# w_in's columns dealt to partitions in runs of four, w_out in two transfers of 8 KB runs, alpha loaded in place

## The chip, the cores and the metric

The kernel runs on one core of one Trainium2 chip. The metric is the device time of one execution in microseconds; the given figure is the median of three runs. A profiled execution of the same kernel gives the trace that is read below.

## The reference

A sparse attention (a window of 32 to each side, and 8 global tokens that see all and are seen by all) is followed by a feed-forward layer with the snake activation. B is 8, there are 8 heads of 64, 576 tokens in each batch element, d_model is 512 and d_ff is 2048.

```python
scores = scale * (q @ k.T)                  # scale = 1 / sqrt(64)
mask = (abs(pos[:, None] - pos[None, :]) <= 32) | is_global[:, None] | is_global[None, :]
attn = softmax(where(mask, scores, -1e9))
x = (attn @ v).transpose(0, 2, 1, 3).reshape(4608, 512)
h = x @ w_in                                # 512 x 2048
g = h + sin(alpha * h) ** 2 / (alpha + 1e-9)
out = g @ w_out                             # 2048 x 512, float32 out
```

All inputs are float32, the indices int64. The kernel computes in bf16 with float32 accumulation.

## The kernel before

The eight batch elements go through three steps each: `attention(b)`, `gemm1(b)` (x times w_in, then the activation) and `gemm2(b)` (the result times w_out, then the store). The order of the instructions on each engine is the order of the program text: nothing is rescheduled. gemm2's matmuls are a generator, and `fill(n)` takes n of them into the stream of PE between the matmuls of the next element's attention and gemm1.

The hidden dimension d_ff is cut into 16 groups of 128, `nt`. In gemm1 a group takes 8 matmuls: 4 chunks `c` of d_model by two halves of the tokens, each with its own weight load of w_in (L992), 288 columns wide (320 for the last element). ACT then computes the sine with `alphaT[:, nt]` as its scale (L1022), ACT or DVE squares it, and DVE adds it to h into `H2` (L1030). gemm2 loads 128 tokens of `H2` as weights and streams 512 columns of `w_out[:, nt]` (L1049).

The weights come in through POOL's queue, which converts float32 to bf16 on the way: `load_w_in` in four quarters of 512 columns (L411; two at the start, two in the first attention step), and `load_w_out` in four transfers of four groups each (L417), issued in gemm1 of element 0 at group 11. Behind `load_w_out` on POOL stand the cast of the global V rows (L696), the copies of the global keys and queries of element 1 into `KX` and `QX` (L372, L377), and the loads of V (L394). A DMA waits until the one eight places ahead of it on its queue has landed.

The hidden unit that group `nt` holds at partition p is `nt * 128 + p`: w_in's columns of a group lie side by side, w_out's rows of a group are 128 rows in order, 2 KB apart in DRAM. `alpha` is loaded by SP as 16 rows of 128 (`arow`, L483), turned by PE (L680) and copied to `alphaT` by ACT (L684). SP's queue goes on with reading the eight indices into registers, gathering the global rows of k (L489), loading the global V rows of element 0 (L403), gathering q, and turning k and q of element 1 (L340). The DVE makes `recipT` from `alphaT` (L1119).

Near the end the kernel judges whether the fast path's limits held: ACT squares w_in (L890), DVE adds the squares into `W2`, PE sums `W2` over its partitions with 16 matmuls of one column (L897, the column norms). At the end the verdict is read into registers by all engines, POOL stores the global rows with an indirect DMA (L1083), 54 matmuls into banks that nothing reads follow on PE (L1199), and each engine jumps over a general path (L1206) that this input does not take.

Of the kernel before, what the change touches and what calls it, by code (L numbers as in the profile page):

```python
# [11 lines left out]
AF = mybir.ActivationFunctionType  # L12
DT = mybir.dt
# [3 lines left out]
P = 128  # L17
# [3 lines left out]
WCOL = 120  # L21
# [5 lines left out]
QROW = QLEN + 2 * PAD  # L27
CUT = 3 * SEG
PLACES = [(w, t, y) for w in (1, 0) for t in range(2) for y in range(2)]
LIM_SUM = float(2.0**50)  # L30
LIM_REC = float(2.0**40)
TINY = float(2.0**-60)
LIM_ARG2 = 9.3


def general_path(tc, q, k, v, global_idx, out, w_in, w_out, alphaT, recipT):


    nc = tc.nc
    B, H, S, D = q.shape  # L40
    NKT = S // KW
    NT = alphaT.shape[1]
    CT = w_in.shape[1]
    DM = w_out.shape[2]
    HALF = S // 2
    WIN = 32
# [7 lines left out]
    with ExitStack() as gx:  # L54
# [4 lines left out]
        idf = one.tile([P, P], DT.float32, name="g_idf")  # L59
# [5 lines left out]
            out=g64[:],  # L65
            in_=bass.AP(tensor=global_idx.tensor, offset=global_idx.offset, ap=[[0, P], [1, NG]]),
# [13 lines left out]
        for j in range(NG):  # L80
            for at, acc in ((pos, colg), (row, rowg)):
                nc.vector.scalar_tensor_tensor(
                    out=acc[:], in0=at[:], scalar=gf[:, j : j + 1], in1=acc[:],
# [5 lines left out]
        for i in range(NKT):  # L89
            for sgn in (1, -1):  # L90
                nc.gpsimd.affine_select(
                    out=MQ[:, i, :], in_=MQ[:, i, :], compare_op=ALU.is_ge, fill=0.0,
# [3 lines left out]
                out=MQ[:, i, :], in0=MQ[:, i, :], scalar1=rowg[0:KW, i : i + 1], scalar2=None,  # L96
# [4 lines left out]
            out=NEG[:], in0=MQ[:], scalar1=1.0, scalar2=1.0e9, op0=ALU.subtract, op1=ALU.mult  # L101
# [5 lines left out]
        with tc.For_i(0, B, 1) as b:  # L107
            for hp in range(H // 2):
                nat = []
                for src, name in ((q, "g_Qn"), (k, "g_Kn"), (v, "g_Vn")):  # L110
                    t = wk.tile([KW, NKT, 2, D], DT.float32, name=name)
                    for h in range(2):
                        nc.sync.dma_start(
                            out=t[:, :, h, :],
                            in_=src[bass.ds(b, 1), 2 * hp + h].rearrange("o (j p) d -> p (o j) d", p=KW),
# [6 lines left out]
                for src, name in ((Qn, "g_qT"), (Kn, "g_kT")):  # L122
                    pt = ps.tile([P, 2, 512], DT.float32, name="g_pt")
                    for i in range(NKT):
                        nc.tensor.transpose(
                            out=pt[:, i // 3, (i % 3) * KW : (i % 3 + 1) * KW],
                            in_=src[:, i, :, :], identity=idf[0:KW, 0:KW],
                        )
                    t = wk.tile([P, S], DT.float32, name=name)
# [6 lines left out]
                for h in range(2):  # L136
                    lo = h * D
                    for i in range(NKT):
                        sp = ps.tile([KW, 2, 512], DT.float32, name="g_sp")
                        for e in range(2):  # L140
                            nc.tensor.matmul(
                                out=sp[:, e, 0:HALF],
# [52 lines left out]
            for nt in range(NT):  # L195
                hg = ps.tile([P, 2, 512], DT.float32, name="g_pt")
                for c in range(CT):
                    for e in range(2):
                        nc.tensor.matmul(
                            out=hg[:, e, 0:HALF], lhsT=w_in[:, c, nt * P : (nt + 1) * P],  # L200
                            rhs=xT[:, c, e * HALF : (e + 1) * HALF],
                            start=(c == 0), stop=(c == CT - 1),
                        )
                y = wk.tile([P, 2, HALF], DT.float32, name="g_y")
                n = wk.tile([P, 2, HALF], DT.float32, name="g_n")
                nc.vector.tensor_scalar(
                    out=y[:], in0=hg[:, :, 0:HALF], scalar1=alphaT[:, nt : nt + 1], scalar2=None,
                    op0=ALU.mult,
                )
                nc.vector.tensor_scalar(  # L210
                    out=n[:], in0=y[:], scalar1=1.0 / TWO_PI, scalar2=None, op0=ALU.mult
                )
                for m in (MAGIC, -MAGIC):
                    nc.vector.tensor_scalar(out=n[:], in0=n[:], scalar1=m, scalar2=None, op0=ALU.add)
                for part in (hi, mid, low):
                    nc.vector.scalar_tensor_tensor(
                        out=y[:], in0=n[:], scalar=-part, in1=y[:], op0=ALU.mult, op1=ALU.add
                    )
                edge = float(np.nextafter(np.float32(np.pi), np.float32(0)))
                nc.vector.tensor_scalar(  # L220
                    out=y[:], in0=y[:], scalar1=edge, scalar2=-edge, op0=ALU.min, op1=ALU.max
                )
                nc.scalar.activation(out=y[:], in_=y[:], func=AF.Sin)
                nc.vector.tensor_tensor(out=y[:], in0=y[:], in1=y[:], op=ALU.mult)
                nc.vector.scalar_tensor_tensor(
                    out=HB[:, nt, :].rearrange("p (e c) -> p e c", e=2),
                    in0=y[:], scalar=recipT[:, nt : nt + 1], in1=hg[:, :, 0:HALF],
                    op0=ALU.mult, op1=ALU.add,
                )
# [18 lines left out]
def kernel(  # L248
# [23 lines left out]
    assert global_idx.shape[0] == NG and NT12 == 12  # L272

    const = ctx.enter_context(tc.tile_pool(name="const", bufs=1))
    w_in = const.tile([P, CT, DFF], DT.bfloat16, name="w_in")
    w_out = const.tile([P, NT, DM], DT.bfloat16, name="w_out")
    alphaT = const.tile([P, NT], DT.float32, name="alphaT")
    recipT = const.tile([P, NT], DT.float32, name="recipT")
# [128 lines left out]

    def load_w_in(gs):
        for g in gs:
            cols = slice(g * DFF // 4, (g + 1) * DFF // 4)  # L410
            nc.gpsimd.dma_start(  # L411
                out=w_in[:, :, cols], in_=moe_w_in[:, cols].rearrange("(c p) n -> p c n", p=P)
            )

    def load_w_out():
        for g in range(4):
            nc.gpsimd.dma_start(  # L417
                out=w_out[:, 4 * g : 4 * g + 4, :],
                in_=moe_w_out[4 * g * P : (4 * g + 4) * P, :].rearrange("(t p) n -> p t n", p=P),
            )  # L420


# [49 lines left out]
        out=g64[:],  # L472
        in_=bass.AP(tensor=global_idx.tensor, offset=global_idx.offset, ap=[[1, NG], [0, B], [1, 1]]),
    )
    arow = setup.tile([NT, P], DT.float32, name="arow")
    nc.sync.dma_start(out=girow[:], in_=global_idx[None, :])
    for t in (0, D):
        nc.sync.dma_start(out=gp64[t + KT : t + KT + NG], in_=global_idx[:, None])
# [1 line left out]
            out=gidx8[t + KT : t + KT + NG],  # L480
            in_=bass.AP(tensor=global_idx.tensor, offset=global_idx.offset, ap=[[0, NG], [1, NG]]),
        )
    nc.sync.dma_start(out=arow[:], in_=moe_alpha.rearrange("(t p) -> t p", p=P))  # L483
    gi32 = girow[:].bitcast(DT.int32)
    greg = [nc.sync.value_load(gi32[0:1, 2 * j : 2 * j + 1], min_val=0, max_val=S - 1) for j in range(NG)]

# [188 lines left out]
    for w, name in ((1, "k"), (0, "q")):  # L675
# [1 line left out]
        nc.tensor.transpose(  # L677
            out=pg[w][:], in_=g0[name][:], identity=identb[0 : NG * B, 0 : NG * B]
        )
    nc.tensor.transpose(out=both[:, 0:NT], in_=arow[:], identity=idf[0:NT, 0:NT])  # L680
    for t in range(2):
        place_global_keys(t, act)
        place_global_queries(t, act)
    act(out=alphaT[:], in_=both[:, 0:NT])  # L684
    turn_part(0, 1, views([z[:] for z in zo]))
    turn_part(1, 1, views([zn[:, n, :] for n in range(2)]))
    def second_half():
# [199 lines left out]
    def square_w(c):  # L887

        t = KX[0][:].rearrange("p h i c -> p (h i c)")[:, (c - 1) * DFF : c * DFF] if c else W2[:]
        nc.scalar.activation(out=t, in_=w_in[:, c, :], func=AF.Square)  # L890
        if c:
            nc.vector.tensor_tensor(out=W2[:], in0=W2[:], in1=t, op=ALU.add)

    def column_norms(pw):

        for nt in range(NT):
            nc.tensor.matmul(  # L897
                out=pw[:, nt : nt + 1], lhsT=W2[:, nt * P : (nt + 1) * P], rhs=ones[:, 0:1],
                start=True, stop=True, skip_group_check=True,
            )  # L900
        c2 = normp.tile([P, NT], DT.float32, name="c2")
        nc.vector.tensor_tensor(out=c2[:], in0=alphaT[:], in1=alphaT[:], op=ALU.mult)
        nc.vector.tensor_tensor(out=c2[:], in0=pw[:, 0:NT], in1=c2[:], op=ALU.mult)
        nc.vector.tensor_reduce(out=limit[:], in_=c2[:], axis=AX.X, op=ALU.max)
        nc.vector.tensor_scalar(
            out=limit[:], in0=limit[:], scalar1=1e-30, scalar2=1.0 / LIM_ARG2, op0=ALU.max, op1=ALU.mult
        )
        nc.vector.reciprocal(out=limit[:], in_=limit[:])
# [60 lines left out]
    def gemm1(b):  # L969
# [11 lines left out]
        def chunks(nt, cs):  # L981
            if nt not in hs:
                if order[nt] == "o":
                    hs[nt] = [(slice(e, e + 1), zo[e][:, None, :]) for e in range(2)]
                else:
                    h = {"n": zn, "d": zd}.get(order[nt]) or hr.tile([P, 2, 512], DT.float32, name="zr")
                    hs[nt] = [(slice(0, 2), h[:])]
            h = [ap[:, i] for es, ap in hs[nt] for i in range(es.stop - es.start)]
            for c in cs:
                for e in range(2):  # L990
                    lhsT = w_in[:, c, nt * P : (nt + 1) * P]
                    nc.tensor.matmul(  # L992
                        out=h[e][:, 0:W], lhsT=lhsT, rhs=xT[:, c, e, 0:W],
                        start=(c == 0), stop=(c == CT - 1), skip_group_check=True,
                    )
# [195 lines left out]
    verdicts = judge(zn[:, 0, :])  # L1191
    next(verdicts)
    sure = gemm2_globals(verdicts)
    tiles = [(r, c) for r in (0, D) for c in (0, D)]
    for kinds, n in ((tiles, 6), (tiles[0:2], 6), (tiles[0::3], 6), ([None], 6)):
        for i in range(n):
            for at in kinds:
                rows, cols = (slice(0, P), slice(0, P)) if at is None else [slice(x, x + D) for x in at]
                nc.tensor.matmul(  # L1199
                    out=(zn if len(kinds) == 2 else zd)[cols, (rows.start or 0) // D, 0:WCOL],  # L1200
                    lhsT=VX[0][rows, 0, i, cols], rhs=H2[rows, i, 0:WCOL],
                    start=True, stop=True, skip_group_check=True,
                )
    mctx.close()

    with tc.If(sure < P, preferred_fallthrough_block=False):  # L1206
# [31 lines left out]
```

## Time and profile before

| | |
|---|---|
| median of 3 runs | 366.73 us (366.41 to 366.94) |
| the profiled execution's own time | 366.15 us |
| its span, first to last instruction | 364.4 us |
| mean granted clock of TensorE | 0.993 |
| PE / ACT / DVE / POOL busy | 338.4 / 293.5 / 283.3 / 139.2 us |
| weight loads of w_in (L992) | 1024, 98 ns each |
| w_in, w_out: transfers | 4 and 4, 512 KB each as written |

In the profile, PE is the matmuls and PEld the weight loads, which overlap the matmuls; the ends of matmuls are modelled, so the distance between starts says more than a single duration. A name such as `zo<-w_out,H` says what is written and what is read. "idle before" is the time in which the engine stood still ahead of an instruction, with what ended it; "issue" means that nothing in the profile explains it. The lines with `SPq` or `POOLq` are instructions of a queue. A line's number is that of the kernel before.

### The profile page before, as it was taken

What the parts mean: (1) busy time and instruction counts of PE and PEld (TensorE: products, weight loads), DVE (VectorE), ACT (ScalarE), POOL (GpSimd) and SP (SyncE); (2) the same over time, 40 slices, a digit from 0 to 9 for tenths busy, and PEclk for the clock granted to TensorE, in tenths of its full rate; (3) what the DMA queues carried; (4) which work ended last, traced back from release to release, by engine and by line L of the source; (5) the groups of instructions that cost most, each with busy time, mean ns of one, the idle gap of its engine ahead of it and who ended that gap; (6) DMA issues with size and microseconds to landing.
All of it is one profiled execution on the core that took longest, in us unless ns stands there. A gap on an engine that the chain in (4) does not pass through costs nothing. (4 is left out here: it accounts for less than half of the span.)

```text
span 364.4 us, 8575 instructions
## 1 busy us (share of the span) xinstructions
PE 338.4 (93%) x3110; PEld 230.8 (63%) x3110; DVE 283.3 (78%) x623; ACT 293.5 (81%) x566; POOL 139.2 (38%) x246
## 2 busy tenths in 40 slices
PE   2579978999999999999999999999999999999994
PEld 1467656766567666776666766766676766655453
DVE  6776998588988877888888887888788866798661
ACT  7689997886978788887888897979888888878711
POOL 7992686669874702661066304730000000000001
PEclk9999998999999999999999999999999999999999
DMA  7997999999999783989199904647120011000321
GB/s 118 120 171 162 181 146 189 156 168 198 146 237 202 73 123 81 172 89 161 31 158 120 149 29 50 68 50 148 43 59 29 2 31 60 29 3 0 105 70 53
DMA packets 103580, 38.07 MB, mean 104 GB/s; under 512 B 94139, under 2 KB 98251, under 8 KB 103083
## 3 DMA queue, kind: packets, MB, share of 16 engines
q0 software_dynamic: 56640, 18.56, 44.6%
q1 hardware_dynamic: 46890, 18.89, 25.5%
q8 instruction: 26, 0.43, 0.5%
q14 instruction: 24, 0.19, 0.2%
HBM read 37.15 MB, written 17.83 MB: 151 GB/s over the span
## 5 line engine op out<-in xcount | busy, mean ns | idle before, releaser
L1049 PE MATMUL zo<-w_out,H 128*128 128x512 bf16 x576 | 153.7, 379 | 0.0
L992 PEld LDWEIGHTS <-w_in 128*128 128x128 bf16 x1024 | 98.6, 98 | 45.6 <-issue 9.1
L394 POOL DMA_DIRECT2D VX<-in_v_dram x128 | 83.3, 659 | 89.8 <-PE zd L784 62.9
L1049 PEld LDWEIGHTS <-H 128*128 128x128 bf16 x576 | 52.3, 97 | 37.2
L750 ACT ACTIVATE E<-ring 128x480 bf16<-128x480 f32 x96 | 54.2, 567 | 22.6 <-PE ring L742 22.2
L753 DVE TENSOR_TENSOR E<-E,MASK 128x480 bf16<-128x480 bf16 x96 | 36.0, 405 | 16.9 <-ACT E L750 15.5
L1083 POOL DMA_INDIRECT out_dram<-osb,ghalf x1 | 1.1, 1067 | 119.6 <-POOLq L1206 119.6
L1030 DVE SCALAR_TENSOR_TENSOR H<-s,recipT,zn 128x576 bf16<-128x576 bf16 x47 | 38.2, 814 | 10.3 <-ACT s L1026 6.5
L1026 ACT ACTIVATE s<-sb 128x576 bf16<-128x576 bf16 (+1 forms) x62 | 42.7, 689 | 2.0
L742 PE MATMUL ring<-QX,KX 128*128 128x120 bf16 x384 | 38.0, 225 | 6.5 <-ACT E L750 3.0
L742 PEld LDWEIGHTS <-KX 128*128 128x128 bf16 x384 | 29.0, 102 | 22.0 <-issue 8.8
L1022 ACT ACTIVATE sb<-zn,alphaT 128x576 bf16<-128x576 f32 (+1 forms) x47 | 34.7, 739 | 9.8 <-PE zn L992 9.7
L1030 DVE SCALAR_TENSOR_TENSOR H<-s,recipT,zd 128x576 bf16<-128x576 bf16 x39 | 31.7, 814 | 6.5 <-ACT s L1026 4.7
L1030 DVE SCALAR_TENSOR_TENSOR H<-s,recipT,zr 128x576 bf16<-128x576 bf16 x39 | 31.7, 813 | 4.5 <-ACT s L1026 2.4
L1022 ACT ACTIVATE sb<-zd,alphaT 128x576 bf16<-128x576 f32 (+1 forms) x39 | 28.9, 740 | 7.1 <-PE zd L992 5.8
L1028 DVE TENSOR_TENSOR s<-sb 128x576 bf16<-128x576 bf16 (+1 forms) x66 | 30.7, 465 | 4.1 <-ACT sb L1022 3.6
L1022 ACT ACTIVATE sb<-zr,alphaT 128x576 bf16<-128x576 f32 (+1 forms) x39 | 28.9, 740 | 5.6 <-PE zr L992 5.4
L784 PEld LDWEIGHTS <-VX 128*128 128x128 bf16 x448 | 26.6, 100 | 9.4 <-issue 3.5
L1055 ACT COPY osb<-zo 128x512 f32<-128x512 f32 x36 | 20.8, 577 | 11.3 <-PE zo L1049 10.0
L992 PE MATMUL zn<-xlast,w_in 128*128 128x288 bf16 (+1 forms) x192 | 28.8, 289 | 0.3
L992 PE MATMUL zn<-xT,w_in 128*128 128x288 bf16 x184 | 26.9, 286 | 2.3 <-DVE H L1030 0.9
L784 PE MATMUL zn<-E,VX 128*128 128x120 bf16 (+2 forms) x336 | 26.9, 211 | 1.0 <-DVE xlast L816 0.9
(163 smaller groups left out, 492.6 us busy)
## 6 DMA issues: line engine op xcount, KB each, us to landing
VX<-in_v_dram POOLq DMA_DIRECT2D x128, 36.0 KB, 5.4
kd<-in_k_dram POOLq DMA_DIRECT2D x7, 576.0 KB, 7.1
qd<-in_q_dram POOLq DMA_DIRECT2D x7, 576.0 KB, 10.1
w_in<-in_moe_w_in_dram POOLq DMA_DIRECT2D x4, 512.0 KB, 6.0
w_out<-in_moe_w_out_dram POOLq DMA_DIRECT2D x4, 512.0 KB, 7.8
out_dram<-osb SPq DMA_DIRECT2D x8, 256.0 KB
out_dram<-osb SPq DMA_DIRECT2D x8, 224.0 KB
out_dram<-osb SPq DMA_DIRECT2D x8, 192.0 KB
```

The lines of the kernel that those rows point to most:

```text
L394: nc.gpsimd.dma_start(out=VX[b % 2][r : r + 24, hp, :, t * D : t * D + D], in_=v[b, 2 * hp + t].rearrange("(i a y) d -> y a i d", a=24, y= ...
L742: nc.tensor.matmul(out=ps[:, e * WCOL : (e + 1) * WCOL], lhsT=kx[:, hp, i, :], rhs=qx[:, hp, :, s0 : s0 + 60], start=True, stop=True, skip ...
L750: nc.scalar.activation(out=Eg, in_=ps[:, 0 : 4 * WCOL], func=AF.Exp, scale=scale, accum_out=EA[:, n : n + 1])
L753: nc.vector.tensor_tensor(out=Eg, in0=Eg, in1=MASK[:, 4 * g : 4 * g + 4, :].rearrange("p i c -> p (i c)"), op=ALU.mult,)
L784: nc.tensor.matmul(out=out_t[:, half, :, a - half * CUT : z - half * CUT], lhsT=OB[:] if key else VXb[:, hp, i, :], rhs=E[:, i, :, a - s0 ...
L992: nc.tensor.matmul(out=h[e][:, 0:W], lhsT=lhsT, rhs=xT[:, c, e, 0:W], start=(c == 0), stop=(c == CT - 1), skip_group_check=True,)
L1022: nc.scalar.activation(out=sb[:, es, 0:W], in_=h[:, :, 0:W], func=AF.Sin, scale=alphaT[:, nt : nt + 1])
L1026: nc.scalar.activation(out=s2[:, :, 0:W], in_=sb[:, :, 0:W], func=AF.Square)
L1028: nc.vector.tensor_tensor(out=s2[:, :, 0:W], in0=sb[:, :, 0:W], in1=sb[:, :, 0:W], op=ALU.mult)
L1030: nc.vector.scalar_tensor_tensor(out=H2[:, nt, r0 : r0 + S].rearrange("p (e c) -> p e c", e=2)[:, es], in0=s2[:, es, 0:HALF], scalar=recip ...
L1049: nc.tensor.matmul(out=ops[:], lhsT=H2[:, nt, blk * P : (blk + 1) * P], rhs=w_out[:, nt, :], start=(nt == 0), stop=(nt == NT - 1),)
L1055: nc.scalar.copy(out=osb[:], in_=ops[:])
```

## The change

There are four edits.

- Partition p of group `nt` now holds the hidden unit `512 * (nt // 4) + 4 * p + nt % 4`. A weight load of w_in takes every fourth column of a quarter (`columns(nt)`), and the tile of w_in is laid out quarter by quarter, `[P, 4, CT, 512]`, each quarter's load writing one block. The square of w_in, the column norms and the general path follow the new layout.
- `load_w_out` takes two transfers in place of four. A partition's four rows of a quarter lie side by side in DRAM, so a run is 8 KB as read and 4 KB as written.
- `alpha` is loaded straight into `alphaT`, in runs of four values; the tile `arow`, its transposition on PE and the copy on ACT go.
- The 54 matmuls ahead of the end of the program are left out.

```diff
+RUN = 4
+def columns(nt):
+    return slice(nt % RUN, nt % RUN + RUN * 127 + 1, RUN)
...
-    w_in = const.tile([P, CT, DFF], DT.bfloat16, name="w_in")
+    w_in = const.tile([P, NT // RUN, CT, RUN * P], DT.bfloat16, name="w_in")
...
     def load_w_in(gs):
         for g in gs:
-            cols = slice(g * DFF // 4, (g + 1) * DFF // 4)
             nc.gpsimd.dma_start(
-                out=w_in[:, :, cols], in_=moe_w_in[:, cols].rearrange("(c p) n -> p c n", p=P)
+                out=w_in[:, g],
+                in_=moe_w_in[:, g * RUN * P : (g + 1) * RUN * P].rearrange("(c p) n -> p c n", p=P),
             )
     def load_w_out():
-        for g in range(4):
+        for half in range(2):
+            rows = slice(half * DFF // 2, (half + 1) * DFF // 2)
             nc.gpsimd.dma_start(
-                out=w_out[:, 4 * g : 4 * g + 4, :],
-                in_=moe_w_out[4 * g * P : (4 * g + 4) * P, :].rearrange("(t p) n -> p t n", p=P),
+                out=w_out[:, half * NT // 2 : (half + 1) * NT // 2, :].rearrange("p (g t) n -> p g (t n)", t=RUN),
+                in_=moe_w_out[rows].rearrange("(g p t) n -> p g (t n)", p=P, t=RUN),
             )
...
-    arow = setup.tile([NT, P], DT.float32, name="arow")
...
-    nc.sync.dma_start(out=arow[:], in_=moe_alpha.rearrange("(t p) -> t p", p=P))
+    nc.sync.dma_start(
+        out=alphaT[:].rearrange("p (g t) -> p g t", t=RUN),
+        in_=moe_alpha.rearrange("(g p t) -> p g t", p=P, t=RUN),
+    )
...
-    nc.tensor.transpose(out=both[:, 0:NT], in_=arow[:], identity=idf[0:NT, 0:NT])
...
-    act(out=alphaT[:], in_=both[:, 0:NT])
...
     def square_w(c):
-        nc.scalar.activation(out=t, in_=w_in[:, c, :], func=AF.Square)
+        nc.scalar.activation(out=t.rearrange("p (g n) -> p g n", n=RUN * P), in_=w_in[:, :, c, :], func=AF.Square)
...
-                out=pw[:, nt : nt + 1], lhsT=W2[:, nt * P : (nt + 1) * P], rhs=ones[:, 0:1],
+                out=pw[:, nt : nt + 1], lhsT=W2[:, nt // RUN * RUN * P :][:, columns(nt)], rhs=ones[:, 0:1],
...
     def gemm1(b):
-                    lhsT = w_in[:, c, nt * P : (nt + 1) * P]
+                    lhsT = w_in[:, nt // RUN, c, columns(nt)]
...
     sure = gemm2_globals(verdicts)
-    tiles = [(r, c) for r in (0, D) for c in (0, D)]
-    for kinds, n in ((tiles, 6), (tiles[0:2], 6), (tiles[0::3], 6), ([None], 6)):
-        for i in range(n):
-            for at in kinds:
-                rows, cols = (slice(0, P), slice(0, P)) if at is None else [slice(x, x + D) for x in at]
-                nc.tensor.matmul(
-                    out=(zn if len(kinds) == 2 else zd)[cols, (rows.start or 0) // D, 0:WCOL],
-                    lhsT=VX[0][rows, 0, i, cols], rhs=H2[rows, i, 0:WCOL],
-                    start=True, stop=True, skip_group_check=True,
-                )
     mctx.close()
```

More of the change, by code (lines that the diff above doesn't have):

```diff
@@ L42, in general_path @@
     NT = alphaT.shape[1]
-    CT = w_in.shape[1]
+    CT = w_in.shape[2]
     DM = w_out.shape[2]
@@ L199, in general_path @@
                         nc.tensor.matmul(
-                            out=hg[:, e, 0:HALF], lhsT=w_in[:, c, nt * P : (nt + 1) * P],
+                            out=hg[:, e, 0:HALF], lhsT=w_in[:, nt // RUN, c, columns(nt)],
                             rhs=xT[:, c, e * HALF : (e + 1) * HALF],
```

## The prediction

> **What bounds the kernel now.** I read the page first, then the busy times by stretch, then the groups of instructions by form, and then the timeline around each place that the change touches.
>
> ```profile
> span 364.4 us, 8575 instructions
> ...
> PE 338.4 (93%) x3110; PEld 230.8 (63%) x3110; DVE 283.3 (78%) x623; ACT 293.5 (81%) x566; POOL 139.2 (38%) x246
> ...
> q1 hardware_dynamic: 46890, 18.89, 25.5%
> ...
> L992 PEld LDWEIGHTS <-w_in 128*128 128x128 bf16 x1024 | 98.6, 98 | 45.6 <-issue 9.1
> ```
> ```profile
> 52.50:60.50 8.00, 5.75 (x61) 4.44 (x62) 7.56 (x21) 6.35 (x15) 6.30 (x12) 0.79 1.33 197
> 60.50:333.00 272.50, 269.79 (x2443) 183.19 (x2440) 219.37 (x446) 229.43 (x447) 92.52 (x169) 1.00 0.67 98
> ```
>
> The columns of the second fence are the stretch, its length, the busy time of PE, PEld, DVE, ACT and POOL, the granted clock, the share of the DMA engines and GB/s. From 60.5 to 333 us PE is busy for 269.8 of 272.5 us at full clock: there the matmul stream is the bound, and only what lengthens PE's stream, or makes it wait, moves the end. Ahead of 60.5 us it is the chain of loads, ACT and DVE. So each part is priced by one question: does it touch PE's stream, or the chain of the first 60 us, or the tail?
>
> **The change part by part.** *Weight loads with a step.* 1024 weight loads of w_in now take columns that lie 4 elements (8 bytes) apart. A weight load lies beside the matmul ahead of it, so its room is the distance between two matmuls.
>
> ```profile
> L992 PE MATMUL zr<-xT,w_in 128*128 128x288 bf16 x152 | 22.4, 286 | 0.0
> ...
> L704 PEld LDWEIGHTS zo<-idf,H 64*128 64x128 f32 x8 | 0.6, 138 | 0.2 <-issue 0.2
> ...
> L897 PE MATMUL zn<-ones,W 128*128 128x1 bf16 x16 | 0.5, 163 | 0.0
> ```
> ```profile
> 45.72 0.57 PEld L704 LDWEIGHTS zo<-idf,H 64*128 64x128 f32 x8 [0.24 <-issue]
> ...
> 287.44 1.14 PE L992 MATMUL zn<-xT,w_in 128*128 128x288 bf16 x8
> ...
> 347.05 0.54 PE L897 MATMUL zn<-ones,W 128*128 128x1 bf16 x16
> ```
> ```profile
>   issue: 9.1, 31
> ...
>   DVE HG L1036: 3.4, 10
> ```
>
> Eight matmuls of 288 columns take 1.14 us, the last one 0.286: they start (1.14 - 0.286) / 7 = 122 ns apart. That is a load's room. What a load occupies when nothing hides it shows in the column norms, whose matmuls have one column: (0.54 - 0.163) / 15 = 25 ns apart, load included. No row has a load with a step. The slowest load here is the f32 one of L704: (0.57 - 0.138) / 7 = 62 ns apart. So the ends are 25 and 62 ns; both are far below 122, and inside gemm1 the cost is 0 either way. It shows in two places only. The 16 loads of the column norms have no cover and stand in PE's stream ahead of the last of gemm2: 0 to 16 x (62 - 25) ns = 0.6 us. And where PE begins again after a wait, the first load's length may be seen: the third fence counts 31 such waits on "issue" and 10 on HG for the loads of w_in, at 0 to 138 - 98 = 40 ns each, so 0 to 1.6 us. I take 0 for both: the stepped load has the type, the rows and the column count of the 25 ns load, and only the step is new.
>
> [...] No row here shows a step.
>
> *alpha in place.* SP now issues 512 runs of 16 bytes in place of 16 runs of 512; one PE transpose and one small ACT copy go.
>
> ```profile
> 3.46 0.32 SPq L483 DMA_DIRECT2D arow<-in_moe_alpha_dram  x1
> ...
> 16.02 0.17 DVE L1119 TENSOR_SCALAR recipT<-alphaT 128x16 f32<-128x16 f32 x1
> ...
> 16.14 0.96 PE L742 MATMUL ring<-QX,KX 128*128 128x120 bf16 x8 [1.45 <-DVE QX L612]
> ...
> 21.84 8.06 SPq L489 DMA_DIRECT2D H<-in_q_dram  x8
> ...
> 32.26 2.16 SPq L340 DMA_TRANSPOSE kt<-kd  x1
> ...
> 42.68 1.15 PE L992 MATMUL zn<-xT,w_in 128*128 128x288 bf16 x8 [0.79 <-DMA w_in<-in_moe_w_in_dram]
> ...
> 43.87 0.74 ACT L1022 ACTIVATE sb<-zn,alphaT 128x576 bf16<-128x576 f32 x1
> ```
> ```profile
> SPq L340 <- DMA kd<-in_k_dram: 3.3, 1, 3.3
> ```
>
> The removed copy saves nothing: the first scores at 16.14 waited for DVE's QX. The new wait is DVE's L1119, first needed at 16.02, over 12 us after the issue; behind it on DVE are the first masks. What is queued behind alpha on SP: eight register loads, three gathers, the loads of the global V rows and the transposes of k and q. SP is done with the gathers at 21.84 + 8.06 = 29.90 and issues the transpose at 32.26 after a wait, so it has 2.36 us to spare. The issue's price: in the low case by the transposes. Of q1's 46890 packets some 12300 are counted in the code for outputs, gathers and global rows, the other 34600 belong to 14 transposes, 2470 each in 2.16 us, so 512 runs add 0.45 us. In the high case by the gathers, 64 runs in 8.06 / 8 = 1.0 us: 8 us. I take the low one, as 128 partitions spread like the transposes' rows, and it is under the 2.36. The packets themselves: q1's mean is 0.255 x 364.4 x 16 / 46890 = 32 ns, so 512 take 512 x 32 / 16 = 1.0 us of all engines, while k, q and V stream in. A delay there passes by way of kd, the transposes and the third load of w_in to the PE wait at 42.68, and ACT's sine at 43.87 follows it at once. Between 0 and 1.0 us; I take 0.2, as most of it falls before V's loads fill the queue.
>
> *w_out in two transfers.* POOL issues two transfers of 256 runs in place of four of 512.
>
> ```profile
> 46.85 3.08 POOL L417 DMA_DIRECT2D w_out<-in_moe_w_out_dram x4 [0.23 <-DMA VX<-in_v_dram]
> ...
> 49.65 0.42 DVE L708 CAST kTg<-zo 128x256 bf16<-128x256 f32 x1
> ...
> 50.48 3.13 POOL L372 COPY KX<-kTg 64x96 bf16<-64x96 bf16 x8
> ...
> 53.84 1.28 ACT L726 ACT_TABLE_LOAD   x1
> ...
> 54.42 0.37 PE L742 MATMUL ring<-QX,KX 128*128 128x120 bf16 x4 [1.96 <-POOL QX L377]
> ...
> 55.14 0.57 ACT L750 ACTIVATE E<-ring 128x480 bf16<-128x480 f32 x1
> ...
> 60.56 0.59 PE L1049 MATMUL zo<-w_out,H 128*128 128x512 bf16 x2
> ...
> 61.20 0.64 POOL L394 DMA_DIRECT2D VX<-in_v_dram  x1 [2.22 <-DMA w_out<-in_moe_w_out_dram]
> ```
>
> POOL saves about 3.08 / 2 = 1.5 us. Behind it stand the copies of the global keys and queries, for which PE waits 1.96 us at 54.42: it looks like a gain of 1.5. But the copies need kTg, which DVE writes until 49.65 + 0.42 = 50.07, so they start at most 50.48 - 50.07 = 0.4 us earlier. And what is late next is ACT: its first exp starts at 55.14, right when the table load ends (53.84 + 1.28 = 55.12), though its scores were done by 54.42 + 0.37 = 54.79. So the path gains 0; bounds -0.4 and 0. The weights are first used at 60.56, and the last of four transfers had landed by 61.20, so the first of two halves is there with room: 0. w_in's loads keep their runs; the squares on ACT keep their sizes: 0.
>
> *The tail.* 54 matmuls that nothing reads go from PE's end.
>
> ```profile
> 356.43 0.35 SPq L1062 DMA_DIRECT2D out_dram<-osb  x1
> ```
> ```profile
> 358.96 0.49 PE L1199 MATMUL zd<-H,VX 128*128 128x120 bf16 x6
> 359.60 1.07 POOL L1083 DMA_INDIRECT out_dram<-osb,ghalf  x1 [119.64 <-POOLq L1206]
> ```
> ```profile
> L1206 PEldq COMPARE_BRANCH  x1: 3297/3297/3297, 359.6 to 359.6; - x1
> ```
> ```profile
> q14 instruction: 3, 0.02, 6.6%
> q0 software_dynamic: 2, 0.00, 1.3%
> ```
> ```profile
> DMA to landing us min/median/max: 3.2/3.2/3.2
> ```
>
> What ends last is POOL's store of the global rows, 359.60 + 3.2 = 362.8, and then the closing semaphores. POOL's queue waits for the earlier stores, the last of which SP issues at 356.43, not for these matmuls: removing them moves the store by 0. But PE's jump over the other path (3.3 us from 359.6, while its code is fetched) starts when they end at 359.45, and would start over a microsecond earlier. The fourth fence is the DMA traffic from 361.8 to 363 us: the store's last two packets run beside three packets of instructions. With PE's fetch out of the way the landing can be 0 to 362.8 - 361.8 = 1.0 us earlier. I take -0.4, near the middle.
>
> **Sum** against the profiled execution, 366.15 us (span 364.4 and 1.75 around it): 0 + 0.2 + 0 - 0.4 = -0.2, so 365.95. The median of the runs is 366.73; with the same difference 366.5. Less than 0.2% (0.73 us) is about what a measurement of this kernel can tell from no change.
>
> **The rivals.** *A: the step takes the fast load away (slower).* Place: the column norms and PE's restarts in gemm1. Price: 0.6 + 1.6 = 2.2 us on top of -0.2, up to 368.7. It decides once a stepped load occupies clearly more than 25 ns. For: f32 loads show 62 against 25 ns. Against: same type and column count. *B: the stepped load is longer than its room.* Beyond 122 ns each further ns costs 1024 ns; at 140 ns it is 18 us, 385. Against: no load here occupies even 63 ns. *C: alpha holds SP.* Beyond 2.36 us of issue everything to the third load of w_in slides; the high case, 8 - 0.3 - 2.4, gives +5.3, 371.8. *D: faster.* The second fence shows a mean clock of 0.79 from 52.5 to 60.5 us, after PE's wait at 54.42. If POOL's 0.4 us keep PE awake, up to 8 x (1 - 0.79) = 1.7 us of slow clock go; with the landing's full 1.0 us the time is near 365. *E: the halves don't land sooner and nothing else moves:* that is the forecast within its bounds.
>
> **How the numbers follow.** Forecast (with E) 0.48, its own range 365.8 to 367.3; A 0.24; B 0.07; C 0.06; D 0.15. A, B and C are slower: 0.37. D and the forecast's lower edge are faster: 0.15 + 0.04 = 0.19. Same: 0.44. The range goes from D's 365.0 to A's 368.8 and leaves out B, most of C and D's far side.
>
> **What would show it.** Right: loads of w_in start 122 ns apart as before and PE is busy as before from 60 to 333 us; the norms' 16 matmuls in 0.54 us; w_out's two issues near 1.5 us in total, and ACT's first exp of the second batch still right behind its table load; PE's jump near 358.5; the last landing 0 to 1 us sooner after the store. Wrong: matmuls of gemm1 further apart than 122 ns (B), the norms longer by 0.6 us (A), the transpose issued after 32.7 (C), a full clock in the stretch from 52 to 60 us (D).

## The result and the profile after

The changed kernel takes 370.88 us (median of 4 runs, 369.97 to 371.24) against 366.57 us for the kernel before (median of 4, 365.97 to 366.94): a ratio of 1.0115, 95% interval 1.0092 to 1.0139. It is 4.3 us slower, outside the predicted range. The profiled execution took 371.24 us, of which 369.5 is the span.

The page of the kernel after, and three groups of instructions of the kinds that the prediction priced (busy us, mean ns of one, idle time before them):

```profile
span 369.5 us, 8461 instructions
...
PE 338.5 (92%) x3055; PEld 245.7 (67%) x3055; DVE 284.1 (77%) x623; ACT 293.2 (79%) x565; POOL 137.7 (37%) x244
...
PEclk9999995899999999999999999999999999999998
...
L999 PEld LDWEIGHTS <-w_in 128*128 128x128 bf16 x1024 | 114.8, 114 | 32.1 <-issue 7.5
...
L424 POOL DMA_DIRECT2D w_out<-in_moe_w_out_dram x2 | 1.4, 718 | 0.1
...
L904 PE MATMUL zn<-ones,W 128*128 128x1 bf16 x16 | 0.7, 171 | 0.0
```

PE is busy for as long as before (338.5 and 338.4 us), although the 54 matmuls at the end, 1.54 us of it before, are left out. So the other matmuls took some 1.7 us longer, and the rest of the 5.1 us more of span is waiting. Placing the same instruction in both traces tells where: the first scores start 0.25 us later than before, the first products of element 1 (`zn<-E,VX`) 2.6 us, the first gemm2 matmul 3.8 us, the last one 4.7 us. Most of it arises between 54 and 65 us. The timeline of the kernel after shows the chain there, with the wait ahead of an instruction in brackets:

```profile
47.19 1.43 POOL L424 DMA_DIRECT2D w_out<-in_moe_w_out_dram  x2
...
54.32 0.37 PE L749 MATMUL ring<-QX,KX 128*128 128x120 bf16 x4 [1.64 <-POOL QX L383]
...
60.92 0.53 PE L791 MATMUL zn<-E,VX 128*128 128x88 bf16 x4 [2.30 <-DMA VX<-VGb]
...
63.06 0.57 ACT L757 ACTIVATE E<-ring 128x480 bf16<-128x480 f32 x1 [4.17 <-PE ring L749]
...
64.39 1.06 PE L1056 MATMUL zo<-w_out,H 128*128 128x512 bf16 x2
```

Before, the same products started without a wait:

```profile
58.28 0.58 PE L784 MATMUL zn<-E,VX 128*128 128x88 bf16 x4
```

`VX<-VGb` is SP's load of the global V rows of element 1, many packets of 128 bytes on queue q1, while w_out comes in on POOL's queue q0. The DMA view from 55 to 58 us, inside w_out's transfer, gives each queue's packets, MB and share of the 16 engines' time; first the kernel before, then the kernel after:

```profile
q0 software_dynamic: 596, 0.59, 117.9%
q1 hardware_dynamic: 284, 0.03, 15.0%
```
```profile
q0 software_dynamic: 151, 0.61, 103.9%
q1 hardware_dynamic: 74, 0.01, 4.0%
```

w_out moves the same bytes (0.59 and 0.61 MB), but in packets of 4096 bytes written in place of 1024. By its record one of them takes 1.039 x 48 / 151 = 0.33 us, before 1.179 x 48 / 596 = 0.095 us (48 is 3 us of 16 engines; the shares add up to more than 100%, so records overlap and these times are a little too long). The small packets fell by the same factor, 284 to 74: in both kernels there are two of w_out's packets to one of theirs, whatever the size.

The trace of the kernel after suggests why it is two. The landing of each small load has 8 reports, that of each w_out transfer 16, read here as one from each engine. In the window 70 of the 71 starts of packets of 128 bytes are followed within 10 ns by the start of one of w_out's, and 80 of w_out's follow none. That reads as one to one on half of the engines, with w_out alone on the others; the engines themselves are inferred, as the trace at hand doesn't name a packet's engine.

That is the theory for the experiments, called W: the two queues take turns on an engine by packet, so four times longer packets on one queue leave the other a quarter of its rate. It is the author's reading of the 284 and 74 small packets; no row shows a turn by itself.

The second thing that the windows show is the clock (the column after POOL). The first row is the kernel before, the other two are the kernel after:

```profile
60.50:67.00 6.50, 5.57 (x65) 3.63 (x62) 3.88 (x11) 5.42 (x17) 5.09 (x9) 1.00 1.52 187
```
```profile
60.50:67.00 6.50, 6.08 (x49) 4.49 (x50) 2.45 (x8) 3.28 (x9) 4.29 (x7) 0.51 1.40 182
...
56.61:66.85 10.24, 7.94 (x58) 5.33 (x56) 6.07 (x19) 5.28 (x17) 6.39 (x11) 0.50 1.36 184
```

From 56.61 to 66.85 us PE ran at half clock, 10.24 us in a row; before, half clock lasted 3.41 us (55.67 to 59.08). In this trace the wait and the slow clock lie together, and the experiments have to part them.

### The profile page after: what moved, and what is told of

It reads as the page before. It is cut to its first block, busy times and chain, and to the rows that moved or that the text cites. A ratio compares the mean times of both kernels' runs of the same rounds, so it can differ in the third digit from the quotient of the medians.

```text
span 369.5 us, 8461 instructions
## 1 busy us (share of the span) xinstructions
PE 338.5 (92%) x3055; PEld 245.7 (67%) x3055; DVE 284.1 (77%) x623; ACT 293.2 (79%) x565; POOL 137.7 (37%) x244
## 3 DMA queue, kind: packets, MB, share of 16 engines
q1 hardware_dynamic: 47386, 18.89, 25.4%
## 5 line engine op out<-in xcount | busy, mean ns | idle before, releaser
L999 PEld LDWEIGHTS <-w_in 128*128 128x128 bf16 x1024 | 114.8, 114 | 32.1 <-issue 7.5
```

The costliest lines, as they stand in the source:

```text
L999: nc.tensor.matmul(out=h[e][:, 0:W], lhsT=lhsT, rhs=xT[:, c, e, 0:W], start=(c == 0), stop=(c == CT - 1), skip_group_check=True,)
```

## Experiments

The rivals to W: S, the stepped weight loads; A, alpha's small pieces; the clock by itself; the tail. Each kernel is compared with the kernel before on the same chip, so ratios count and not single times.

**w_out's transfers alone.**

```diff
 (the kernel before)
-        for g in range(4):      # 2 KB runs, four transfers
+        for half in range(2):   # 8 KB runs, two transfers, as in the change
...
```

> The kernel before with one part of the change, load_w_out in two transfers of 8 KB runs; w_in's columns stay as before, so the rows of w_out that meet an element of zn are not its own, and only the time is read. Theory W (w_out's packets of 4096 B and the small packets of SP's loads of the global values take turns on each DMA engine, so that the small ones fall from 284 to 74 between 55 and 58 us, and PE waits for them): the whole loss is here, 370.0 to 371.0 us against 366.6, some 75 small packets in 55 to 58, and PE waits of 2 to 3 us for VX<-VGb ahead of zn<-E,VX near 58 to 61. Rival S (the stepped weight loads of gemm1 and the norms cost it): 366.3 to 366.9 here. Rival A (alpha's load in 2048 pieces holds SP or the DMA engines): the same, 366.3 to 366.9.

Ratio 1.0131 (1.0107 to 1.0154), 371.22 against 366.35 us: the whole loss, a little more than expected, without any other part of the change. The DMA view from 55 to 58 us and the timeline:

```profile
q0 software_dynamic: 168, 0.62, 104.4%
q1 hardware_dynamic: 75, 0.01, 3.9%
```
```profile
61.45 0.53 PE L786 MATMUL zn<-E,VX 128*128 128x88 bf16 x4 [3.05 <-DMA VX<-in_v_dram]
```

75 small packets, as expected. PE waits 3.05 us at the same place. The releaser is named as V's own load here and `VX<-VGb` in the kernel after; both write `VX`, and the name is only what ended last by the profile. What speaks for VGb is the time of its packets: the first 192 of them (heads 0 and 1) have started by 60.73 us here and by 60.03 in the kernel after, 0.7 and 0.9 us ahead of the products; before it was 57.08 us. SP's own queue is closer still: its tenth load waits for the second, that of head 1, to land (the last report is 0.02 us ahead of the tenth's issue, in the kernel before and in the kernel after). It is issued at 61.33 us here and at 60.80 in the kernel after, and the products start 0.12 us later both times (before: 57.67, and the products 0.61 us later). The pieces of V that land here at the same time belong to head pairs 2 and 3 (`load_v(1, (2, 3))`), which these products don't read.

**The steps alone.**

```diff
 (the kernel before)
-                    lhsT = w_in[:, c, nt * P : (nt + 1) * P]
+                    lhsT = w_in[:, nt // RUN, c, columns(nt)]
...
```

> The kernel before with w_in held quarter by quarter and its columns taken in steps of four, in gemm1 and in the norms; w_out, alpha and the last matmuls stay as before, so the elements of zn don't meet their own rows of w_out or their own alpha, and only the time is read. Theory W: 366.5 to 367.0 against 366.6: gemm1's matmuls still start 122 ns apart though the loads take 114 ns instead of 98, and only the norms' 16 matmuls grow by some 8 ns each. Rival S: 369.5 to 371, the whole loss.

Ratio 1.0028 (1.0003 to 1.0052): 0.1 to 1.9 us. Its profiled span is 364.6 us against 364.4, at the low end of this (it was the fastest of the twelve executions), and the last gemm2 matmul starts 0.3 us later than before. The steps cost little, by these numbers not nothing; they aren't the loss.

**Everything of the change, but w_out in four transfers again, with packets as small as before.**

```diff
 (the kernel after)
-        for half in range(2):
+        for t in range(RUN):
...
-                out=w_out[:, half * NT // 2 : (half + 1) * NT // 2, :].rearrange("p (g t) n -> p g (t n)", t=RUN),
-                in_=moe_w_out[rows].rearrange("(g p t) n -> p g (t n)", p=P, t=RUN),
+                out=w_out[:].rearrange("p (g t) n -> p t g n", t=RUN)[:, t],
+                in_=moe_w_out.rearrange("(g p t) n -> t p g n", p=P, t=RUN)[t],
```

> The kernel after with w_out in four transfers of 2 KB runs, one for each step of four rows, everything else as after. Theory W: the packets are again 1024 B written, the small ones come back to 250 to 290 in 55 to 58 us, PE's wait for VX<-VGb goes, and the time is 366.5 to 367.3, where up to 0.7 us may be left if a gemm2 matmul now waits for the fourth transfer. Rivals S and A: 370.5 to 371.2, as after.

Ratio 0.9993 (0.9975 to 1.0012): the loss is gone, with the steps, alpha and the shorter tail still in. The DMA view from 55 to 58 us, and the products, which start without a wait:

```profile
q0 software_dynamic: 601, 0.60, 118.8%
q1 hardware_dynamic: 283, 0.03, 14.9%
```
```profile
57.38 0.36 PE L788 MATMUL zn<-E,VX 128*128 128x88 bf16 x4
```

**The dose between: 4 KB runs,** two transfers as in the change, `w_out[:].rearrange("p (g u t) n -> p u g (t n)", u=2, t=2)[:, u]`.

> The kernel after with w_out in two transfers of 4 KB runs, everything else as after. Theory W, as a dose: packets of 2048 B written take about 170 to 190 ns, small ones fall to 130 to 160 in 55 to 58 us, and the time lies between the two kernels, 367.5 to 369.5. Rivals S and A: 370.5 to 371.2, as after. If it is the number of transfers (two in place of four) and not the size of the packets, also as after.

Ratio 1.0045 (1.0022 to 1.0068), between the two. Window 55 to 58 us, and the products' wait:

```profile
q0 software_dynamic: 301, 0.62, 109.2%
q1 hardware_dynamic: 147, 0.02, 7.9%
```
```profile
59.51 0.36 PE L788 MATMUL zn<-E,VX 128*128 128x88 bf16 x4 [1.57 <-DMA VX<-VGb]
```

The packets take 1.092 x 48 / 301 = 0.17 us and the small ones fall to half. With two transfers each, the smaller packets lose less, so the size of a packet counts by itself. The number of transfers isn't without effect: some 0.7 us at the end of the program go with it (see the tail), which leaves 0.9 of the 1.6 us here. Packets, time of one, small packets and result stand in one row: 1024 B, 0.095 us, 284; 2048 B, 0.17 us, 147, +0.45%; 4096 B, 0.33 us, 74, +1.15%.

**alpha alone** (no transpose, no copy; the pieces loaded straight into `alphaT`).

> The kernel before with alpha loaded in place (pieces of four values, no transpose and no copy); w_in's columns stay as before, so the values of alpha stand at other columns than their own, and only the time is read. Theory W: 366.4 to 367.0 against 366.6, since the first scores of after started only 0.25 us later than before. Rival A: 1 us or more over before.

Ratio 1.0002 (0.9981 to 1.0023): no difference seen, at most 0.8 us. SP's issue of it takes 0.42 us in place of 0.32. There are 512 pieces (q1 has 47386 packets, 496 more than before), not the 2048 that the first expectation gives.

```profile
3.46 0.42 SPq L483 DMA_DIRECT2D alphaT<-in_moe_alpha_dram  x1
```

**The tail alone.**

> The kernel before without the 54 matmuls behind the last gemm2 column, nothing else changed. The prediction took 0.4 us off for them (bounds 1.0 and 0). In the profile after, the time from the last store to the last instruction is 5.17 us against 4.78, so the other reading is +0.4: 366.2 if the forecast holds, 367.0 if PE's jump now fetches later and POOL's drain ends last.

Ratio 0.9983 (0.9968 to 0.9997), 365.37 against 365.86 us: 0.1 to 1.2 us faster, as the prediction had it. Its profiled span is 1.4 us shorter, but 0.8 of that is there at the last gemm2 matmul already (356.72 against 357.56 us), ahead of what was left out. The closing instructions of POOL in the kernel before, the kernel after and this one:

```profile
L1233 POOLq DRAIN  x3: 46/115/3267, 360.0 to 364.1; - x3
```
```profile
L1230 POOLq DRAIN  x3: 46/115/3907, 364.7 to 369.2; - x3
```
```profile
L1223 POOLq DRAIN  x3: 46/115/2754, 359.1 to 362.8; - x3
```

The longest of these three DRAINs (ns; min, median and max) begins 0.4 us after POOL issues its last store and ends after the store has landed. Over all the traces its length goes with two things:

- The landing. The store landed 2.6 to 2.8 us after its issue in the eight traces without the 54 matmuls, and 3.1 to 3.9 us after it in the five with them. That fits the gain.
- The number of w_out's transfers. The long DRAIN ends 0.46 us after the landing in all seven traces with four transfers, and 1.49 to 1.65 us after it in all six with two, whatever the size of the packets. What follows it, up to the end of the program, is 0.3 us shorter with two (0.84 us for 1.12), so some 0.7 us of the loss lie here, behind the last store, and are not W's. Why the number matters there stays open.

**w_out queued behind the small loads.** In the kernel after, `load_w_out()` moves behind `cast_globals_v()` and `place_globals(1)`.

> The kernel after with load_w_out issued behind the casts and the placing of element 1's global values instead of ahead of them, so SP's small loads start before w_out's packets are queued. Theory W: the early small loads run free, but w_out is queued some 3 to 5 us later and the last small loads still meet it; PE's wait for VX<-VGb shrinks to under 1.5 us, while the first gemm2 may wait for w_out: 367.0 to 370.0. Rivals S and A: 370.5 to 371.2.

Ratio 1.0129 (1.0103 to 1.0154): no better, against the expectation. The small loads now run free and the products don't wait, but w_out is issued at 54.35 us and comes too late. PE's waits from 50 to 95 us:

```profile
PE zo L1056 <- DMA w_out<-in_moe_w_out_dram: 3.9, 2, 2.2
PE ring L749 <- POOL QX L383: 2.2, 1, 2.2
```

The same amount has become a wait for the other transfer. In these two orders neither load had room to let the other go first; sharing the engines in small packets served both (ratio 0.9993 with packets of 1024 bytes).

**Work for the clock in the wait.** The kernel after, with six matmuls that nothing reads ahead of the products.

```diff
+                if b == 1 and hp == 1:
+                    warm(zo[0], 6)
```

> The kernel after with six matmuls that nothing reads put on PE ahead of the products of element 1's second pair of heads, where PE waits for SP's small loads. If a part of the loss is the halved clock (10.24 us from 56.6 on in after, 3.4 us in before) and this work keeps the clock up, 369.3 to 370.2 is expected, with the wait for VX<-VGb unchanged; if the clock is only a companion of the wait, or the matmuls don't reach, 370.6 to 371.2; if the clock were the whole cause, 367.

Ratio 1.0072 (1.0047 to 1.0096), more than expected: some 1.6 us of the 4.3 go (1.0115 less 1.0072, each uncertain by 0.9 us). From 60.5 to 67 us the clock is full:

```profile
60.50:67.00 6.50, 5.57 (x86) 4.34 (x86) 2.95 (x9) 4.28 (x12) 4.64 (x8) 1.00 1.16 164
```

```profile
60.41 0.36 PE L791 MATMUL zn<-E,VX 128*128 128x88 bf16 x4 [0.89 <-DMA VX<-VGb]
```

The products start at 60.41 us in place of 60.92 (w_out's first packet was 0.9 us earlier in this execution), so the wait is still there, filled with matmuls: SP's tenth load goes at 60.29, again 0.12 us ahead of them. That about a third of the loss is the clock and most of the rest the wait fits these numbers, but it isn't shown. In the profile of w_out alone the half clock lasted 3.41 us (61.17 to 64.58), no longer than before, and the loss was as large: the wait there was longer. So the long half clock isn't needed for the loss.

**The same work ahead of the scores.** Seven such matmuls at the start of element 1's attention, once on the version with 2 KB runs, once on the kernel before.

> The kernel with w_out in four transfers of 2 KB runs (else as after), plus seven matmuls that nothing reads, on PE at the start of element 1's attention, where it waits for POOL's query copies. In three of the runs the clock is halved for 3.41 us from about 55 us on, right behind that wait; in three others (2 KB runs, 4 KB runs, alpha alone) it isn't, and these reach the last gemm2 column 0.8 to 1.0 us earlier than the trend. If the wait is what halves it, all executions keep the full clock there: 365.0 to 365.6 against some 366.2 for before, and no half-clock stretch between 50 and 70 us. If not, 365.8 to 366.2, as without them.

> The kernel before with those seven matmuls alone, nothing else changed. If the wait halves the clock: 365.3 to 365.9 against some 366.2, the half-clock stretch at 55.7 gone from the profile. If not, 366.0 to 366.5.

Ratios 0.999 (0.9954 to 1.0026) and 1.0011 (0.9984 to 1.0039): no gain. Neither profile shows a half clock before 361 us. With 2 KB runs there was none without the matmuls either, so only the kernel before bears on whether the wait halves the clock: 3.41 us of half clock without the matmuls and none with them, in one profile each. The version with alpha alone had no half clock there without such matmuls either, so the cause isn't shown. The price set on the slow clock was wrong. On the kernel before, the time went into a new wait:

```profile
58.21 0.36 PE L784 MATMUL zn<-E,VX 128*128 128x88 bf16 x4 [0.79 <-DMA VX<-VGb]
```

The products start at 58.21 us, against 58.28 with the slow clock, and SP's tenth load goes at 58.09, 0.12 us ahead of them. The small loads are the bound at this place even with 1024-byte packets; the slow clock in the kernel before was hidden under them.

**The small loads dealt over two queues** (the kernel after; even heads from SP, odd heads from ACT).

> The kernel after, with element 1's loads of global values dealt over two queues: the even heads from SP as before, the odd heads from ACT at the start of element 1's attention. Theory W with turns by queue: each of the two queues gets its turn between w_out's packets, so that small packets rise from 74 to 120 to 150 in 55 to 58 us though w_out's packets stay 4096 B; PE's wait for VX<-VGb shrinks, while ACT pays four issues ahead of its first exponential: 368.5 to 370.5 against 370.9 for after. If w_out's packets hold the engines for their bytes and turns don't go by queue, the count stays at 70 to 85, the wait stays 2 to 3 us, and the time is 371 to 373.

Ratio 1.0139 (1.0104 to 1.0173), 371.39 us, and 77 packets on q1 from 55 to 58 us, none on ACT's queue: ACT issued its first load at 54.75, but the queue's packets started only at 58.86 us, when w_out was nearly done. So it doesn't tell whether a third queue gets turns of its own. It shows that the issue of such a load is some 4 us from its first packet in this stretch. The products, at 61.20 us, didn't wait for `VX` here; ACT was late, as its first exponential started behind the issues at 58.06 us, against 55.55 in the kernel after.

## Why the prediction was wrong

- **w_out in two transfers: forecast 0 (bounds -0.4 and 0), measured +4.8 us alone (ratio 1.0131), of which some 0.7 us lie in POOL's closing steps.** This is the step that failed: "the first of two halves is there with room: 0". It looked at POOL's order and at w_out's own landing, and both held: the issue fell from 3.08 to 1.43 us, the copies of the global keys started at 50.43 us against 50.48, and the first gemm2 matmul didn't wait for w_out. It did not ask which other queue has packets on the same engines in that window, though the page shows q1. With turns by packet, which no row shows by itself, the price could have been estimated beforehand from the kernel before: the products need 192 small packets, 284 in 3 us make that 2.0 us, and at a quarter of the rate 8 us, cut short only because w_out ends near 60 us (its last packet starts at 59.87 us in the kernel after). Measured, from the first to the 192nd, it was 2.2 us before (54.85 to 57.08) and 5.7 us after (54.29 to 60.03).
- **Rivals.** None of them was this mechanism. Rival D had the clock in the right stretch with the wrong sign: it would have gained 1.7 us by keeping PE awake, but with the seven matmuls on the kernel before the clock was full there, and nothing was gained (ratio 1.0011). In the kernel after the slow clock was longer instead (10.24 us against 3.41).
- **Stepped loads: forecast 0, bounds 0.6 and 1.6 us.** The pace of gemm1 held, with loads of 114 ns in place of 98: eight matmuls still take 1.14 us.

```profile
288.29 1.14 PE L999 MATMUL zn<-xT,w_in 128*128 128x288 bf16 x8
...
351.66 0.66 PE L904 MATMUL zn<-ones,W 128*128 128x1 bf16 x16
```

  The norms took 0.66 us in place of 0.54: (0.66 - 0.171) / 15 = 33 ns apart, against 25 before and 62 in rival A's bound, 0.1 us in all. So a step does cost something. The steps alone measured +0.1 to +1.9 us; the profile of it shows only the low end, and what the rest would be stays open. "Waits on issue" of the kernel after are fewer, 7.5 against 9.1 us, so the term for restarts isn't seen.
- **alpha: forecast +0.2 (0 to 1.0).** Within the bounds: alone it can't be told from nothing.
- **The tail: forecast -0.4 (-1.0 to 0).** Alone 0.6 us faster by the ratio, interval 0.1 to 1.2. The reason given, instructions fetched beside the store, fits: without the matmuls PE's jump begins 1.3 us ahead of the store (357.42 and 358.76 us), with them as the store is issued (359.64 and 359.60), and the store lands sooner in every trace without them. That the fetch is the cause was not tested.
- **The sum of the parts.** Measured alone they are +4.8, +1.0, 0.1 and -0.6, together +5.3, each uncertain by up to 0.9 us; the whole change measured +4.3. With w_out's packets small, and in four transfers, the rest of the change comes to -0.3 us, interval -0.9 to +0.4.

Of the versions run, the kernel before without the last 54 matmuls is the only one whose interval lies below 1, by 0.17% (0.03 to 0.32).

## What to carry to other kernels

Before making a transfer's runs longer, look in the DMA view at who else has packets in the same window: here large packets were paid by the small ones on the other queue, about in proportion to their time (0.095, 0.17 and 0.33 us each left 284, 147 and 74 small ones in 3 us), although the large transfer's landing (60.91 us before, 60.61 after) and the total rate (209 and 208 GB/s) hardly changed. Price such an edit at the consumer of the small transfer, not of the large one. And where a wait grows ahead of PE, look at the clock too: with w_out alone the half clock began at 61.17 us, in the wait of 3.05 us that ended at 61.45; in the kernel after it began at 56.61 us, ahead of the wait of 2.30 us, and lasted 10.24 us.

## What the hardware showed that was not expected

- Two queues shared the engines by packets and not by bytes: two of w_out's packets to one small one at 1024, 2048 and 4096 bytes (596 to 284, 301 to 147, 151 to 74). The landing of a small load had 8 reports and that of a w_out transfer 16, and the rows read as one to one on half of the engines.
- The larger packets brought no speed: 0.59, 0.62 and 0.61 MB of w_out in the same 3 us.
- A weight load of every fourth column took 114 ns in place of 98, and 33 ns in place of 25 where nothing covered it.
- The half clock lasted 3.41 us in the kernel before and 10.24 us, three times as long, in the kernel after, where the wait for `VX` fell inside it. With six matmuls in that wait it was 3.41 us again, from 54.52 us on, ahead of the wait; with w_out alone it was 3.41 us without them.
- POOL's last DRAIN ended 0.46 us after its store had landed in seven traces with four transfers of w_out, and 1.49 to 1.65 us after it in six with two.
